# Scores in 32x64 tiles of 64 keys for five of eight chunks, and a late scaling in the first chunk

## The chip, the cores and the metric

The kernel runs on one core of a Trainium2 chip. The metric is device time in microseconds (us), the median of several executions. TensorE (PE; its weight loads are the profile's PEld) multiplies, VectorE (DVE), ScalarE (ACT) and GpSimd (POOL) work beside it, and SyncE (SP) issues the DMAs.

## What is computed

Two layers, each attention and an MLP, on 2048 tokens of 576 features. Attention has 32 heads of 18 features; a query sees itself and the 255 keys before it.

```python
def _A_ref(x, wqkv, wo):
    H = 32; Dh = D // H; W = 256
    qkv = (x @ wqkv).reshape(B, S, 3, H, Dh).transpose(2, 0, 3, 1, 4)
    scores = einsum("bhqd,bhkd->bhqk", q, k) * Dh ** -0.5
    mask = (i - j >= 0) & (i - j < W)
    return (softmax(where(mask, scores, -1e9)) @ v) ... @ wo
def _B_ref(x, w1, b1, w2, b2):
    return gelu(layernorm(x) @ w1 + b1) @ w2 + b2
x = x + _A_ref(layernorm(x)); x = x + _B_ref(layernorm(x)); both once more
```

## The kernel before

**Chunks and stages.** The work is cut into eight chunks of 512 tokens (four blocks of 128): chunks 0 to 3 are layer 1, chunks 4 to 7 layer 2. Attention of chunk k is interleaved with the MLP of chunk k - 1. A chunk's scores, exps, masks and P V products form three stages (`ea`, `eb`, `ec`) of 3, 3 and 2 of the 8 head groups (`CUTS`, line 566); the matmuls of the MLP and of the projections fill TensorE between them.

**Scores.** A head group is four heads, each on its own 32 partitions of `qT` and `kT`. `scores` (L946, its matmuls on L957) takes keys as the stationary side, 128 of them, and streams up to 384 queries; the four heads run as four 32x128 tiles at once. One call is a burst of 512 columns for each head, written into two pairs of PSUM banks. A chunk with a chunk before it needs three bursts for a head group: 1536 columns, in which 128x128 blocks on the edge of the mask are computed in full. Two exps on ScalarE (L964, 1024 elements per partition each) empty a burst into one of six slots of `pT`; GpSimd cuts the masked blocks to zero (affine_select, L984); `pv` (L991, matmuls on L1002) multiplies with V in four 128x32 tiles. Chunks 0 and 4 have no chunk before them and need fewer columns.

**Tile shapes.** Between such bursts TensorE works in other shapes: 64x128 in L880, L1085 and L1130, 128x128 in L821 and L840, 128x32 in L824 and L1002. `quad` (L819) writes the same product either as one wide 128x128 matmul (L821) or as four 128x32 ones (L824).

**Chunk 0.** Its LayerNorm (`ln_norm_T`, L756) subtracts the mean and multiplies by the reciprocal deviation `rstd` in one VectorE instruction (L761). `rstd` comes from GpSimd (L749, L751). With `pe=True`, TensorE transposes the row (L778) and ScalarE copies it out (L781). The projections follow (L840), and their results leave PSUM by copies on VectorE (L888, L901) or ScalarE (L898).

**What sets the order.** `Plan` collects tasks with the tensors that they read and write; the table `ORDER` gives each engine its tasks by number, in the order in which they are issued, and `BANKS` the PSUM bank of each. `schedule` (L248) turns them into queues with semaphores; it also chooses `wide` for `quad` and puts warming matmuls (L726) into gaps. Every engine issues in its written order.

Of the kernel before, what the change touches and what calls it, by code (L numbers as in the profile page):

```python
# [361 lines left out]
PACE = {"f": 16.0, "c": 65.0, "r": 100.0, "h": 18.5, "s": 33.0}  # L362
# [8 lines left out]
def spread(s):  # L371
    for x in s.split():
# [181 lines left out]
def build_kernel(nc, A_x, A_wqkv, A_wo, B_x, B_w1, B_b1, B_w2, B_b2, out):  # L554
    D = 576
# [24 lines left out]
    NQN = 6  # L580
    WB = 6
    TOPF = D - 512
    KF = 2


    CH = [(l, t, 4) for l in range(NL) for t in range(0, NT, 4)]
# [777 lines left out]
```

## Time and profile before

| | |
|---|---|
| median of 3 runs | 856.53 us (855.35 to 856.9) |
| span of the profiled execution | 853.7 us |
| median less that span | 2.8 us |
| PE / ACT / DVE / POOL busy | 842.8 / 598.3 / 383.2 / 368.6 us |
| matmuls recorded | 11549 |
| granted TensorE clock | 1.000 |

In rows of groups, the two numbers behind the first bar are the busy time in us and the mean duration in ns, and behind the second bar stands the idle time of the engine just before, with what ended it. In rows of a timeline the first two numbers are start and length in us, merged over the instructions counted by x; brackets hold the idle time before them. A shape such as 32\*128 is the tile: rows of the array, then columns.

### The profile page before, as it was taken

What the parts mean: (1) busy time and instruction counts of PE and PEld (TensorE: products, weight loads), DVE (VectorE), ACT (ScalarE), POOL (GpSimd) and SP (SyncE); (2) the same over time, 40 slices, a digit from 0 to 9 for tenths busy, and PEclk for the clock granted to TensorE, in tenths of its full rate; (3) what the DMA queues carried; (4) which work ended last, traced back from release to release, by engine and by line L of the source; (5) the groups of instructions that cost most, each with busy time, mean ns of one, the idle gap of its engine ahead of it and who ended that gap; (6) DMA issues with size and microseconds to landing.
All of it is one profiled execution on the core that took longest, in us unless ns stands there. A gap on an engine that the chain in (4) does not pass through costs nothing.

```text
span 853.7 us, 26814 instructions
## 1 busy us (share of the span) xinstructions
PE 842.8 (99%) x11549; PEld 513.0 (60%) x11549; DVE 383.2 (45%) x943; ACT 598.3 (70%) x736; POOL 368.6 (43%) x551
## 2 busy tenths in 40 slices
PE   9999999999999999999999999999999999999998
PEld 6555555656556566565566665766556656556556
DVE  7877224635237533564237633654324434153013
ACT  5888886968767678578734788548876688862740
POOL 3865644455245473166501763425644256332100
PEclk9999999999999999999999999999999999999999
DMA  9588376361594643936466636575447645254820
GB/s 227 82 159 184 127 203 153 76 190 41 171 173 94 187 136 93 194 56 159 144 196 118 160 83 168 64 191 118 132 137 157 164 118 157 101 178 119 292 84 28
DMA packets 181989, 119.76 MB, mean 140 GB/s; under 512 B 107504, under 2 KB 181872, under 8 KB 181872
## 3 DMA queue, kind: packets, MB, share of 16 engines
q1 hardware_dynamic: 181872, 118.05, 54.7%
q8 instruction: 91, 1.49, 0.7%
q14 instruction: 26, 0.21, 0.1%
HBM read 90.10 MB, written 2.36 MB: 108 GB/s over the span
## 4 chain that ended last, share of the span: by engine, by line
PE 95%; DVE 2%; ACT 1%; DMA 1%; issue 1%; POOL 0%; DVEq 0%
PE ps L1130 33%; PE ps L821 28%; PE ps L880 9%; PE ps L824 8%; PE ps L957 7%; PE ps L1002 5%; PE ps L1085 4%; PE ps L840 2%; ACT pT L964 1%; DMA xnTa<-xn 1%; DVE st_all L736 0%; DVE x_res L1067 0%; DVE xn L761 0%; DMA x_res<-in_A_x_dram 0%; DVE oq L1008 0%
## 5 line engine op out<-in xcount | busy, mean ns | idle before, releaser
L964 ACT ACTIVATE pT<-ps 128x1024 bf16<-128x1024 f32 (+1 forms) x372 | 346.0, 998 | 76.8 <-PE ps L957 76.1
L984 POOL TENSOR_SCALAR_AFFINE_SELECT pT<-pT 128x512 bf16<-128x512 bf16 (+2 forms) x360 | 278.7, 801 | 198.7 <-ACT pT L964 196.8
L1130 PE MATMUL ps<-xnTm,w_sb 64*128 64x512 bf16 x2592 | 291.1, 376 | 0.2 <-ACT pT L964 0.2
L1140 ACT ACTIVATE hT<-ps,b1col 128x512 bf16<-128x512 f32 x276 | 169.6, 690 | 141.6 <-PE ps L1130 141.1
L821 PE MATMUL ps<-w_sb,hT 128*128 128x288 bf16 x1626 | 215.2, 287 | 0.8 <-issue 0.8
L1130 PEld LDWEIGHTS ps<-xnTm,w_sb 64*128 64x128 bf16 x2592 | 125.2, 94 | 144.7 <-issue 6.1
L821 PEld LDWEIGHTS ps<-w_sb,hT 128*128 128x128 bf16 x1626 | 151.5, 98 | 56.1 <-issue 16.3
L1067 DVE TENSOR_TENSOR x_res<-ps,x_res 128x288 f32<-128x288 f32 x224 | 97.0, 449 | 166.5 <-PE ps L821 129.4
L1008 DVE STREAM_TRANSPOSE oq<-ps 128x512 f32<-128x512 f32 x64 | 45.8, 715 | 110.4 <-PE ps L1002 108.9
L880 PE MATMUL ps<-wqkv,xnTa 64*128 64x288 bf16 x1296 | 90.7, 283 | 1.1 <-DMA xnTa<-xn 0.6
L901 DVE CAST qn<-ps 128x288 bf16<-128x288 f32 x114 | 48.3, 449 | 91.5 <-PE ps L880 85.0
L880 PEld LDWEIGHTS ps<-wqkv,xnTa 64*128 64x128 bf16 x1296 | 61.5, 94 | 29.3 <-issue 2.7
L749 POOL TENSOR_SCALAR vtmp<-mv_all 128x1 f32<-128x1 f32 (+1 forms) x43 | 9.0, 209 | 153.4 <-DVE mv_all L740 141.3
L824 PE MATMUL ps<-w_sb,hT 128*32 128x288 bf16 x1944 | 68.3, 287 | 0.0
L957 PE MATMUL ps<-qT,kT 32*128 32x256 bf16 (+2 forms) x1248 | 63.0, 273 | 1.2 <-ACT pT L964 0.8
L824 PEld LDWEIGHTS ps<-w_sb,hT 128*32 128x32 bf16 x1944 | 49.6, 97 | 11.9 <-issue 4.2
L1145 POOL TENSOR_TENSOR x_res<-x_res,b2bc 128x576 f32<-128x576 f32 x32 | 40.7, 1286 | 35.1 <-ACT hT L1140 35.1
L888 DVE CAST vA<-ps 128x288 bf16<-128x288 f32 x64 | 27.5, 447 | 61.1 <-PE ps L880 58.9
L736 DVE BATCH_NORM_STATS2 st_all<-x_res 128x6 f32<-128x288 f32 (+1 forms) x128 | 53.3, 442 | 3.4 <-DMA x_res<-in_A_x_dram 3.2
L1002 PE MATMUL ps<-pT,vA 128*20 128x384 bf16 (+2 forms) x1440 | 50.1, 273 | 0.1
L957 PEld LDWEIGHTS ps<-qT,kT 32*128 32x128 bf16 x1248 | 19.2, 92 | 39.8 <-issue 20.6
L1085 PE MATMUL ps<-wo_sb,attT 64*128 64x288 bf16 x576 | 40.2, 283 | 0.9 <-DVE qn L901 0.5
(57 smaller groups left out, 462.0 us busy)
## 6 DMA issues: line engine op xcount, KB each, us to landing
w_sb<-in_B_w_dram SPq DMA_DIRECT2D x46, 864.0 KB, 6.1
w_sb<-in_B_w_dram SPq DMA_DIRECT2D x48, 768.0 KB, 5.7
w_sb<-in_B_w_dram SPq DMA_DIRECT2D x96, 48.0 KB, 3.6
out_dram<-x_res SPq DMA_DIRECT2D x16, 144.0 KB, 4.2
wqkv<-in_A_wqkv_dram SPq DMA_DIRECT2D x3, 576.0 KB, 5.0
x_res<-in_A_x_dram SPq DMA_DIRECT2D x3, 576.0 KB, 4.4
wqkv<-in_B_w_dram SPq DMA_DIRECT2D x2, 864.0 KB, 8.6
wo_sb<-in_A_wo_dram SPq DMA_DIRECT2D x4, 144.0 KB, 3.9
```

The costliest lines, as they stand in the source:

```text
L736: add("dve", lambda e, i=i, s=s: e.bn_stats(st_all[:, t, i, :], s[:, t, i * HB:(i + 1) * HB]), reads=res, writes=[f"st{t}_{i}"], cost=0.37 ...
L821: return e.matmul(bank(b)[:, 0:HB], lhs, rhs, start=start, stop=stop, skip_group_check=True)
L824: ins = e.matmul(bank(b)[32 * j:32 * j + 32, 0:HB], lhs[:, 32 * j:32 * j + 32], rhs, start=start, stop=stop, tile_position=(0, 32 * j), sk ...
L880: ins = e.matmul(bank(bs[o])[:, 0:HB], xnTa[r:r + 64, c, i * 128:(i + 1) * 128], wqkv[r:r + 64, c, col:col + HB], start=(c == 4), stop=(ph ...
L957: ins = e.matmul(two(bs[j // 2])[:, j % 2, col:col + nq * 128], k_of(T0 + so)[0][32 * j:32 * j + 32, g, :], qs[32 * j:32 * j + 32, g, qo * ...
L964: add("act", lambda e, h2=h2: e.activation(pT[:, sl, 2 * h2:2 * h2 + 2, lo:hi], two(bs[h2])[:, :, lo:hi], ACT.Exp, scale=SCALE), reads=[bs ...
L984: add("pool", lambda e, ap=ap, pat=pat, sgn=sgn, kind=kind: e.affine_select(ap, ap, pattern=pat, compare_op=(ALU.is_ge if kind == "d" else ...
L1002: ins = e.matmul(bank(bo)[32 * j:32 * j + VW, qo * 128:(qo + nq) * 128], vA[:, (T0 + so) % VS, 8 * j + g, :], pT[:, sl, j, col:col + nq * ...
L1067: add("dve", lambda e: e.tensor_tensor(x_res[:, t, sl], bank(b)[:, 0:HB], x_old[:, t, sl], ALU.add), reads=[b] + ([f"xin{t}"] if first els ...
L1085: ins = e.matmul(bank(bs[o])[:, 0:HB], attT[r:r + 64, c, i * 128:(i + 1) * 128], wo_sb[r:r + 64, c, o * HB:o * HB + HB], start=(c == 4), s ...
L1130: ins = e.matmul(bank(bks[i])[:, 0:n], w1_sb[r:r + 64, sls[i], col:col + 128], xnTm[r:r + 64, k % 2, c, 0:n], start=(c == 4), stop=(ph == ...
L1140: add("act", lambda e, ff=ff, hd=hd, bk=bk: e.activation(hd[:, 0:n], bank(bk)[:, 0:n], ACT.Gelu_apprx_tanh, bias=b1col[:, ff:ff + 1]), rea ...
```

## The change

**Scores.** For chunks 2, 3, 5, 6 and 7 (`HALF`) a new function `pair` treats two head groups at once. `halves` writes their scores in five bursts of 512 columns instead of six. A tile is now 32x64: half a key block is stationary, so each half meets only the 64-query steps that its own mask leaves, and two halves times four heads make eight tiles. A piece is four matmuls (one per head) with one half of keys. Two bursts of a pair hold four pieces, three hold six. An exp now empties a window of a burst into its place in `pT` (`exps`): 28 exps for a pair, 64 to 384 columns of two banks each, instead of 12. `cut` issues the same masks as before. Waits between exps, masks and P V go by cells of 64 columns (`cells`). The stages now hold 4, 2 and 2 head groups, and score pairs, projections and P V may use any PSUM bank.

**Chunk 0.** With `pe=True` the VectorE instruction only subtracts the mean; the drains behind the projections multiply by `rstd` (VectorE tensor_scalar or ScalarE mul) where they copied.

**Orders.** `ORDER` and `BANKS` are written anew. TensorE has 12490 matmuls instead of 11549. SP loads the tokens of chunk 1 ahead of the k weights.

The diff, cut to its core:

```diff
-    CUTS = ((0, 3, 6, 8), (0, 4, 8, 8))
+    CUTS = ((0, 4, 6, 8), (0, 4, 8, 8))
+    HALF = (2, 3, 5, 6, 7)
-    FILL = (7, 6, 5, 4)
-    OUT = (7, 6, 5, 4)
+    FILL = (7, 6, 5, 4, 3, 2, 1, 0)
+    OUT = (7, 6, 5, 4, 3, 2, 1, 0)
-    SC = (0, 2, 4)
+    SC = (0, 1, 2, 3, 4, 5, 6)
...
+        if pe:
+            add("dve", lambda e: e.tensor_scalar(xn[:, sl, 0:D], s[:, t, :], mv_all[:, t, 0:1], None, op0=ALU.subtract),
+                reads=res + [f"mv{t}"], writes=[f"xn{sl}"], cost=0.37, lat=0.14, prio=prio, port=True)
...
+        def drain(e, dst, src):
+            if k:
+                return e.tensor_copy(dst, src)
+            return e.tensor_scalar(dst, src, rstd[:, i:i + 1], None, op0=ALU.mult)
...
+    def exps(sl, bs, dst, src, n, prio):
+
+        for h2 in range(2):
+            add("act", lambda e, h2=h2: e.activation(pT[:, sl, 2 * h2:2 * h2 + 2, dst:dst + n], two(bs[h2])[:, :, src:src + n], ACT.Exp, scale=SCALE),
+                reads=[bs[h2]], writes=cells(sl, dst, dst + n, (h2,)), cost=0.07 + 2 * n * 0.00083, lat=0.17, prio=prio)
...
+    def halves(k, pieces, wins, prio):
...
+        def fn(e):
+            ins = None
+            for (g, so, u, q, n, col) in pieces:
+                for j in range(4):
+                    ins = e.matmul(two(bs[j // 2])[64 * u:64 * u + 64, j % 2, 64 * col:64 * (col + n)],
+                                   k_of(T0 + so)[0][32 * j:32 * j + 32, g, 64 * u:64 * u + 64], qs[32 * j:32 * j + 32, g, 64 * q:64 * (q + n)],
+                                   start=True, stop=True, tile_position=(32 * j, 64 * u), skip_group_check=True)
+            return ins
...
+        def edge(g, more):
+            unit(g, [(g, 0, 0, 0, 5, 1), (g, 0, 1, 1, 5, 2), (g, 3, 1, 7, 1, 7), (g, 3, 0, 6, 2, 6), (g, -2, 0, 0, 1, 0), (g, -2, 1, 0, 2, 0)],
+                 [(g, "X", 0, 6, 1), (g, "X", 6, 2, 0), (g, "Y", 0, 2, 6)], [(g, "X", "d", 0, 1), (g, "X", "o", 256, 2)] + more)
+        edge(a, [])
+        unit(a, [(a, 1, 0, 2, 5, 3), (a, 1, 1, 3, 4, 4), (a, -1, 1, 0, 4, 0), (a, -1, 0, 0, 3, 0)],
+             [(a, "Y", 2, 5, 3), (a, "Z", 0, 4, 0)], [(a, "Y", "d", 0, 2), (a, "Z", "o", 128, 1)])
+        unit(a, [(a, 2, 0, 4, 4, 0), (a, 2, 1, 5, 3, 1), (b, -1, 1, 0, 4, 4), (b, -1, 0, 0, 3, 4), (a, 1, 1, 7, 1, 0), (b, 1, 0, 2, 1, 7)],
+             [(a, "Z", 4, 4, 0), (a, "Y", 7, 1, 0), (b, "Z", 0, 4, 4), (b, "Y", 2, 1, 7)],
+             [(a, "Z", "d", 256, 1), (a, "Y", "o", 384, 1), (b, "Z", "o", 128, 1)])
+        done(a)
+        unit(b, [(b, 1, 0, 3, 4, 0), (b, 1, 1, 3, 5, 0), (b, 2, 0, 4, 4, 4), (b, 2, 1, 5, 3, 5)],
+             [(b, "Y", 3, 5, 0), (b, "Z", 4, 4, 4)], [(b, "Y", "o", 384, 1), (b, "Z", "d", 256, 1)])
+        edge(b, [(b, "Y", "d", 0, 2)])
+        done(b)
```

A piece is (head group, key block, half of keys, first query, number of queries, column), the last three in steps of 64; a window is (head group, slot, first column there, number, first column of the burst).

Three places of the order show it. First TensorE in attention stage `ea` of chunk 2, before: bursts of chunk 2 (L957) between MLP matmuls of chunk 0 (L821, L824).

```order
L957 MATMUL ps<-qT,kT 128x384 x4
L957 MATMUL ps<-qT,kT 128x128 x4
L821 MATMUL ps<-w_sb,hT 128x288 x18
L957 MATMUL ps<-qT,kT 128x384 x4
L957 MATMUL ps<-qT,kT 128x128 x4
L821 MATMUL ps<-w_sb,hT 128x288 x12
L957 MATMUL ps<-qT,kT 128x256 x8
L824 MATMUL ps<-w_sb,hT 32x288 x24
```

The same stage now (L1037 are the new bursts, L840 and L843 the MLP's wide matmuls and quads), the third to the fifth burst of the first pair:

```order
L1037 MATMUL ps<-qT,kT 64x320 x4
L1037 MATMUL ps<-qT,kT 64x256 x8
L1037 MATMUL ps<-qT,kT 64x192 x4
L840 MATMUL ps<-w_sb,hT 128x288 x12
L1037 MATMUL ps<-qT,kT 64x256 x4
L1037 MATMUL ps<-qT,kT 64x320 x4
L1037 MATMUL ps<-qT,kT 64x256 x4
L1037 MATMUL ps<-qT,kT 64x192 x4
L840 MATMUL ps<-w_sb,hT 128x288 x18
L1037 MATMUL ps<-qT,kT 64x320 x8
L1037 MATMUL ps<-qT,kT 64x64 x4
L1037 MATMUL ps<-qT,kT 64x128 x4
```

Bursts of 8 matmuls became bursts of 16 or 24. With the burst just ahead of these rows and the next one behind them, five bursts in a row stand with 66 wide matmuls (18, 12, 18 and 18), 72 quads and one P V group of 24.

ScalarE at the same place (L978 are the exps; before, its row in the stage was L964 with 128x1024 and x18):

```order
L978 ACTIVATE pT<-ps 128x2x384
L978 ACTIVATE pT<-ps 128x2x128
L978 ACTIVATE pT<-ps 128x2x384
L978 ACTIVATE pT<-ps 128x2x128 x3
L978 ACTIVATE pT<-ps 128x2x64
L978 ACTIVATE pT<-ps 128x2x256
L978 ACTIVATE pT<-ps 128x2x64
L978 ACTIVATE pT<-ps 128x2x256
```

One kind of exp became windows of different widths, each for two banks.

TensorE at the start, before: warming matmuls (L726), transposes of the first rows (L778), projections (L840).

```order
L726 MATMUL ps<-warm 128x256 x13
L778 MATMUL ps<-ident,xn 128x128 x5
L726 MATMUL ps<-warm 128x256 x5
L778 MATMUL ps<-ident,xn 128x128 x5
L840 MATMUL ps<-wqkv,xnTa 128x288 x20
L778 MATMUL ps<-ident,xn 128x128 x5
L840 MATMUL ps<-wqkv,xnTa 128x288 x25
```

And now (L741, L797, L859):

```order
L741 MATMUL ps<-warm 128x256 x8
L797 MATMUL ps<-ident,xn 128x128 x5
L741 MATMUL ps<-warm 128x256 x7
L797 MATMUL ps<-ident,xn 128x128 x10
L859 MATMUL ps<-wqkv,xnTa 128x288 x25
L797 MATMUL ps<-ident,xn 128x128 x4
L859 MATMUL ps<-wqkv,xnTa 128x288 x5
```

The third row of tokens is transposed ahead of the first projection instead of behind 20 of its matmuls, and the first 30 projections are q alone.

More of the change, by code (lines that the diff above doesn't have):

```diff
@@ L361 @@
 RING = 2048
-PACE = {"f": 16.0, "c": 65.0, "r": 100.0, "h": 18.5, "s": 33.0}
+PACE = {"f": 16.0, "c": 65.0, "r": 100.0, "h": 18.5, "s": 33.0, "q": 160.0}
+HALF_EXTRA = 0.05
 FETCH = 300
@@ L960, in scores @@
         rd = [f"{qname}{qo + i}" for (g, so, qo, nq, col) in parts for i in range(nq)] + [k_of(T0 + p[1])[1] for p in parts]
-        add("pe", fn, reads=rd, writes=bs, cost=sum(mm_cost(p[3] * 128) for p in parts), prio=prio, lat=0.15, alloc=bs, mode="r", after=[f"p{sl}h{h}" for h in range(2)] + [f"p{sl}m{m}" for m in range(3)])
         lo, hi = min(p[4] for p in parts), max(p[4] + p[3] * 128 for p in parts)
-        for h2 in range(2):
-            add("act", lambda e, h2=h2: e.activation(pT[:, sl, 2 * h2:2 * h2 + 2, lo:hi], two(bs[h2])[:, :, lo:hi], ACT.Exp, scale=SCALE),
-                reads=[bs[h2]], writes=[f"p{sl}h{h2}"], cost=0.07 + 2 * (hi - lo) * 0.00083, lat=0.17, prio=prio)
+        add("pe", fn, reads=rd, writes=bs, cost=sum(mm_cost(p[3] * 128) for p in parts), prio=prio, lat=0.15, alloc=bs, mode="r", after=cells(sl, lo, hi))
+        exps(sl, bs, lo, lo, hi - lo, prio)
         blk = {}
@@ L978, in scores @@
                 runs.append([blk[c], c, 1])
-        need = {}
-        for mi, (kind, col, nb) in enumerate(runs):
-            sgn = 1 if kind == "d" else -1
-            pat = [[0, 4]] + ([[0, nb]] if nb > 1 else []) + [[sgn, 128]]
-            ap = pT[:, sl, :, col:col + nb * 128]
-            add("pool", lambda e, ap=ap, pat=pat, sgn=sgn, kind=kind: e.affine_select(
-                ap, ap, pattern=pat, compare_op=(ALU.is_ge if kind == "d" else ALU.is_gt), fill=0.0, base=0, channel_multiplier=-sgn),
-                reads=[f"p{sl}h0", f"p{sl}h1"], writes=[f"p{sl}m{mi}"], cost=0.12 + 0.475 * nb, prio=prio)
-            for n in range(nb):
-                need[col + n * 128] = f"p{sl}m{mi}"
-        return sl, {p[4]: [f"p{sl}h0", f"p{sl}h1"] + list(dict.fromkeys(need[c] for c in range(p[4], p[4] + p[3] * 128, 128) if c in need)) for p in parts}
+        for kind, col, nb in runs:
+            cut(sl, kind, col, nb, prio)
+        return sl
+    def halves(k, pieces, wins, prio):
+        l, t0, nt = CH[k]
+        T0 = l * NT + t0
+        qs, qname = q_of(k)
+        bs = [Bank(SC, True), Bank(SC, True)]
+        def fn(e):
[6 more added lines that the diff above has]
+            return ins
+        rd = list(dict.fromkeys([f"{qname}{x // 2}" for (g, so, u, q, n, col) in pieces for x in range(q, q + n)] + [k_of(T0 + p[1])[1] for p in pieces]))
+        add("pe", fn, reads=rd, writes=bs, cost=512 / 2400.0 + 0.0023 * (len(pieces) / 2) + HALF_EXTRA, prio=prio, lat=0.15, alloc=bs, mode="q",
+            after=[c for (sl, dst, n, src) in wins for c in cells(sl, 64 * dst, 64 * (dst + n))])
+        for (sl, dst, n, src) in wins:
+            exps(sl, bs, 64 * dst, 64 * src, 64 * n, prio)
     def pv(k, g, todo, prio):
@@ L999, in fn @@
             ins = None
-            for n, ((_, so, qo, nq, col), sl, _) in enumerate(todo):
+            for n, ((_, so, qo, nq, col), sl) in enumerate(todo):
                 for j in range(4):
@@ L1005, in fn @@
             return ins
-        rd = list(dict.fromkeys([x for _, _, names in todo for x in names] + [f"v{(T0 + p[1]) % VS}h{o}" for p, _, _ in todo for o in range(2)]))
-        add("pe", fn, reads=rd, writes=[bo], cost=sum(mm_cost(p[3] * 128) for p, _, _ in todo), prio=prio, lat=0.2, mode="c", alloc=[bo])
+        rd = list(dict.fromkeys([x for p, sl in todo for x in cells(sl, p[4], p[4] + p[3] * 128)] + [f"v{(T0 + p[1]) % VS}h{o}" for p, _ in todo for o in range(2)]))
+        add("pe", fn, reads=rd, writes=[bo], cost=sum(mm_cost(p[3] * 128) for p, _ in todo), prio=prio, lat=0.2, mode="c", alloc=[bo])
         add("dve", lambda e: e.transpose(oq[:, 0:4 * nt, :].rearrange("p b c -> p (b c)"), bank(bo)[:, 0:nt * 128]),
@@ L1027, in pv, with pair, at, unit @@
                     reads=[f"aq{x}" for x in range(32 * c // DH, g + 1)] + (["ax0", "ax1"] if c == KD - 1 else []), writes=[f"aT{c}"], cost=0.6, lat=0.14, prio=prio - 3)
+    def pair(k, a, b, prio):
+        ss = {}
+        PARTS = {"X": ((0, 0, 3, 0), (-2, 0, 1, 384)), "Y": ((1, 1, 3, 128), (3, 3, 1, 0)), "Z": ((-1, 0, 2, 0), (2, 2, 2, 256))}
+        def at(g, w):
+            if (g, w) not in ss:
+                ss[g, w] = slots.popleft()
+            return ss[g, w]
+        def unit(g, pieces, wins, cuts):
+            PL.part = f".{g}"
+            halves(k, pieces, [(at(x, w), dst, n, src) for (x, w, dst, n, src) in wins], prio)
+            for (x, w, kind, col, nb) in cuts:
+                cut(at(x, w), kind, col, nb, prio)
+        def done(g):
+            pv(k, g, [((g,) + p, ss[g, w]) for w in "XYZ" for p in PARTS[w]], prio - 0.1)
+            for w in "XYZ":
+                slots.append(ss[g, w])
+        def edge(g, more):
[12 more added lines that the diff above has]
+        done(b)
+        PL.part = ""
     def E(k, gs, prio):
+        if k in HALF:
+            for n in range(0, len(gs), 2):
+                pair(k, gs[n], gs[n + 1], prio)
+            return
         todo = units_of(k, gs)
@@ L1048, in E @@
             PL.part = f".{u[0][0]}"
-            sl, names = scores(k, u, prio)
+            sl = scores(k, u, prio)
             flush()
@@ L1052, in E @@
             for p in u:
-                parts[p[0]].append((p, sl, names[p[4]]))
+                parts[p[0]].append((p, sl))
                 left[p[0]] -= 1
```

60 lines of the change are left out of this document (36 added, 24 removed), and 323 rows, old and new, of the table ORDER.

## The prediction

> **What bounds the kernel now.** I read the busy line of the page first, then the chain of work that ended last, then the engines' busy time by stretches.
>
> ```profile
> PE 842.8 (99%) x11549; PEld 513.0 (60%) x11549; DVE 383.2 (45%) x943; ACT 598.3 (70%) x736; POOL 368.6 (43%) x551
> PE 95%; DVE 2%; ACT 1%; DMA 1%; issue 1%; POOL 0%; DVEq 0%
> ...
> 0.00:20.00 20.00, 18.42 (x155) 13.19 (x155) 14.46 (x44) 11.46 (x20) 7.93 (x23) 1.00 1.01 234
> 20.00:100.00 80.00, 75.69 (x1135) 45.27 (x1138) 55.00 (x138) 68.25 (x94) 54.86 (x85) 1.00 0.69 141
> 100.00:800.00 700.00, 698.08 (x9850) 420.14 (x9844) 303.77 (x739) 503.45 (x604) 305.79 (x443) 1.00 0.54 140
> 800.00:853.70 53.70, 50.60 (x428) 34.45 (x424) 9.97 (x24) 15.16 (x22) 0.00 (x0) 1.00 0.33 108
> ```
>
> The window rows give the stretch, its length, then the busy time of PE, PEld, DVE, ACT and POOL. TensorE is busy 842.8 of 853.7 us, and 95% of the chain is its own. Between 100 and 800 us it idles 1.9 us in all; the other 9 us lie in the first 100 us and in the last 53. The granted clock is 1.00 in every row. So whatever happens after 100 us counts only if it changes TensorE's own work, or makes another engine late enough that TensorE must stop. Anything saved on ScalarE (70%), VectorE (45%) or GpSimd (43%) is worth nothing there.
>
> What that work costs is read from starts, not from durations, because matmuls overlap. The timeline rows show start, length, engine, line, tile shape and count:
>
> ```profile
> 330.18 0.40 PE L957 MATMUL ps<-qT,kT 32*128 32x384 bf16 x8
> 330.51 1.64 PE L821 MATMUL ps<-w_sb,hT 128*128 128x288 bf16 x12
> 332.09 0.40 PE L957 MATMUL ps<-qT,kT 32*128 32x384 bf16 x8
> ...
> 333.99 0.40 PE L957 MATMUL ps<-qT,kT 32*128 32x256 bf16 x8
> 334.32 0.83 PE L1002 MATMUL ps<-pT,vA 128*20 128x384 bf16 x24
> 334.98 0.91 PE L824 MATMUL ps<-w_sb,hT 128*32 128x288 bf16 x24
> 335.82 0.40 PE L957 MATMUL ps<-qT,kT 32*128 32x384 bf16 x8
> ...
> 803.28 11.93 PE L821 MATMUL ps<-w_sb,hT 128*128 128x288 bf16 x96
> 815.14 11.83 PE L1130 MATMUL ps<-xnTm,w_sb 64*128 64x512 bf16 x108
> ```
>
> Ninety-six wide matmuls take 815.14 - 803.28 = 11.86 us, twelve take 332.09 - 330.51 = 1.58. The slope is (11.86 - 1.58)/84 = 0.122 us for one, and what is left of the twelve is 1.58 - 12 x 0.122 = **0.11 us for the change of tile shape** behind them. The 24 P V matmuls (334.32 to 334.98) take 0.66 us and pay no such change, since the quads behind them have the same 128-row, 32-column tiles; their streaming alone, 2 x (384 + 128 + 256) columns with four tiles abreast, is 0.64 us at 2.4 columns per ns (the 288 columns of a wide matmul in 0.122 us give that rate). A score burst of 512 columns takes 330.51 - 330.18 = 0.33 us whatever follows it, so **0.22 us and a change**.
>
> **The change part by part.** Sums are made against the profiled execution: 853.7 us of span, 2.8 us below the median of 856.5; I carry that difference along.
>
> *Fewer bursts.* Five chunks x 8 head groups x 3 = 120 bursts of 32x128 tiles become 5 x 4 pairs x 5 = 100 of 32x64 tiles, each still 512 columns wide if its two column halves stream side by side. 20 x 0.22 = **-4.4 us**.
>
> *Fewer changes of shape.* Counted along TensorE's order, neighbours with different tile shapes stand at 410 places before and at 387 now. 23 x 0.11 = **-2.5 us**. Wide matmuls and quads change places (1898 wide and 2104 quad matmuls before, 1956 and 1872 now), at no cost: 24 quads take 335.82 - 334.98 - 0.11 = 0.73 us, as six wide ones do.
>
> *Thicker bursts.* A new burst holds 16 or 24 short matmuls where there were 8. The trace has no 32x64 tile, so this is bounded by the nearest rows.
>
> ```profile
> 330.18 0.12 PEld L957 LDWEIGHTS ps<-qT,kT 32*128 32x128 bf16 x8 [0.24 <-issue]
> ...
> 368.93 0.40 PE L957 MATMUL ps<-qT,kT 32*128 32x128 bf16 x12
> 369.26 1.64 PE L821 MATMUL ps<-w_sb,hT 128*128 128x288 bf16 x12
> ...
> L957 PEld LDWEIGHTS ps<-qT,kT 32*128 32x128 bf16 x1248 | 19.2, 92 | 39.8 <-issue 20.6 <-ACT pT L964 15.5 <-DVE x_res L1067 0.9
> ```
>
> From below: a burst of chunk 4 in three parts and 12 matmuls takes 0.33 us too, so more and shorter parts can be free: 0. From above: the third part on a tile must have its weights loaded after the second part has begun to stream, and one load lasts 92 ns. In the two edge bursts of a pair (queries 320, 64 and 128 wide on one half) that would end at 320/2.4 + 92 + 128/2.4 = 278 ns instead of 213, which is 65 more; in the others 11 at most. That is 32 ns on average. In between lies the program's order: matmuls start in order here, and in an edge burst the last 128 columns stand behind a 64-column piece that begins at column 448, so they end at 576 instead of 512, 27 ns later, 11 ns on average over the five. I add 14 ns because eight first matmuls start one after another instead of four: eight loads take 0.12 us where one takes 92 ns, so starts are about 4 ns apart. I take **25 ns x 100 = +2.5 us**, between the two ends, nearest to the order. What speaks against more is the three-part row.
>
> The Trainium skill has a rule against such a cut: "TensorEngine Tiling (Array Packing)", section "Instruction Overhead", gives each matmul about 60 cycles whatever its width, and advises not to take the tiling factor from a small dimension. The narrowest piece here is 64 columns, just above that, so by the rule the sum stays where it is; the trace shows no piece below 128 columns in a score burst.
>
> *More exps.* A pair's 12 exps become 28 with the same columns. ScalarE's pitch:
>
> ```profile
> 339.65 1.94 ACT L964 ACTIVATE pT<-ps 128x1024 bf16<-128x1024 f32 x2 [1.43 <-PE ps L957]
> ...
> 36.19 10.66 ACT L964 ACTIVATE pT<-ps 128x768 bf16<-128x768 f32 x15 [0.84 <-PE ps L957]
> ...
> 349.30 1.27 ACT L1140 ACTIVATE hT<-ps,b1col 128x512 bf16<-128x512 f32 x2 [3.78 <-PE ps L1130]
> 352.81 0.69 ACT L1140 ACTIVATE hT<-ps,b1col 128x512 bf16<-128x512 f32 x1 [2.25 <-PE ps L1130]
> ...
> L964 ACT ACTIVATE pT<-ps 128x1024 bf16<-128x1024 f32 x324 | 310.8, 1023 | 72.7 <-PE ps L957 72.4
> L964 ACT ACTIVATE pT<-ps 128x768 bf16<-128x768 f32 x48 | 35.2, 828 | 4.1 <-PE ps L957 3.7
> ```
>
> One 1024-element exp behind another costs 1.94 - 1.02 = 0.92 us, a 768-element one (10.66 - 0.83)/14 = 0.70: 0.85 ns per element and 0.05 us fixed. A pair then costs 12288 x 0.85 ns + 28 x 0.05 = 11.8 us against 11.0 before, and the 320 added instructions 16 us of ScalarE in all. The cover is TensorE's work between the bursts. In the stretch of the new order shown for chunk 2, five bursts in a row, with 28 exps, stand with 66 wide matmuls, 72 quads, 24 P V matmuls and ten changes: 5 x 0.245 + 66 x 0.122 + 18 x 0.122 + 0.66 + 1.1 = 13.2 us. ScalarE fits, with 1.4 us to spare, so **0**. If the fixed part is larger than (13.2 - 10.4)/28 = 0.10 us, the cover is gone; that is a rival below. GpSimd's cuts keep number and shape (244, 112 and 4): 0.
>
> *Chunk 0.* Centring no longer waits for the deviation, so the first two rows of tokens reach TensorE sooner. But the q weights land late:
>
> ```profile
> 2.18 4.17 SPq L676 DMA_DIRECT2D wqkv<-in_A_wqkv_dram  x7
> ...
> wqkv<-in_A_wqkv_dram SPq DMA_DIRECT2D x3, 576.0 KB, 5.0
> ...
> 6.60 0.43 DVE L761 TENSOR_SCALAR xn<-x_res,mv_all,rstd 128x576 bf16<-128x576 bf16 x1 [1.03 <-POOL rstd L751]
> ...
> 7.09 0.51 PE L778 MATMUL ps<-ident,xn 128*128 128x128 bf16 x5 [0.40 <-DVE xn L761]
> 7.54 0.49 PEld L840 LDWEIGHTS ps<-wqkv,xnTa 128*128 128x128 bf16 x5
> ```
>
> Issued at 2.18, landing 5.0 us later, they are there at about 7.2 us, and the first projection loads its tokens, the stationary side, at 7.54. What comes off (1.03 us of wait for the second row) is thus shut in by a DMA that stays where it was. The new order also puts the third row's transposes ahead of the projections, and x for chunk 1 ahead of the k weights in SP's queue; the k projections move behind all q ones, which gives back that delay. What is late next is the DMA: **0**, with 1 us either way. Five fewer warming matmuls only filled idle time.
>
> ```profile
> 4.33 0.57 POOL L751 TENSOR_TENSOR rstd<-vtmp,nhalf 128x1 f32<-128x1 f32 x1
> ...
> 8.39 0.46 DVE L901 CAST qn<-ps 128x288 bf16<-128x288 f32 x1
> ...
> L901 DVE CAST qn<-ps 128x288 bf16<-128x288 f32 x114 | 48.3, 449 | 91.5 <-PE ps L880 85.0 <-PE ps L821 3.3 <-PE ps L840 1.8
> ...
> L761 DVE TENSOR_SCALAR xn<-x_res,mv_all,rstd 128x576 bf16<-128x576 bf16 x16 | 7.0, 450 | 1.4 <-POOL rstd L751 1.4
> ```
>
> The drains of chunk 0 now wait for the deviation, with the next statistics and drains of VectorE queued behind them. GpSimd has the first at 4.90 us, the first drain comes at 8.39, so 3.5 us cover that wait. A scaled drain out of PSUM is not in the trace; the same 288 elements copied take 0.45 us and a scaled row of 576 out of memory 0.45, so I count 0, at most 18 x 0.1 us of a VectorE that is busy 72% of the first 20 us.
>
> Sum: -4.4 - 2.5 + 2.5 = **-4.4 us**, 853.7 to 849.3 of span, and **852.1 us** for the median.
>
> **The rivals.** *Loads of one row group go one after another (slower).* A burst of six pieces then needs six loads per row group. The quads bound one load from above: 24 loads of 32 columns in 0.73 us are 30.5 ns each, 61 ns for 64 columns. Six take 366 ns against 220, four take 244: (3 x 146 + 2 x 24)/5 = 97 ns per burst, +9.7 us, 856.5 - 6.9 + 9.7 = **859.3 us**. It decides from 69 ns per burst (6.9 us over 100), about 55 ns a load. For it: every load that shares rows in this trace is narrow. Against: the three-part burst, three loads per row group, shows nothing. The Trainium skill, "TensorE: Matmul & The Clock Gate", section "LDWEIGHTS (loading the stationary operand)", counts a load by its columns, 53 ns for 64, and lets loads overlap only across row groups; by that estimate six take 320 ns and the sum would come out near no change, 856 us. No run here shows such a load yet; that outcome lies in the no-change case below.
>
> *Column halves do not stream side by side where rows are cut too (slower).* +0.213 us per burst: 852.1 - 2.5 + 21.3 = **871 us**. The trace has four row groups abreast (scores) and four column groups abreast (P V), never both.
>
> *ScalarE becomes the pace (slower).* With gelu's fixed part, 1.27 - 0.69 - 512 x 0.85 ns = 0.145 us, a pair costs 14.5 us against 13.2 of TensorE; with two such pairs in each of five chunks +13 us, **865 us**. For exps the two rows above say 0.05.
>
> *The burst eats the gain (no change).* At 52 to 86 ns per burst the time is within 0.2% of before.
>
> *More than forecast.* Bursts as cheap as the three-part row and 1 to 2.5 us fewer waits in the first 100 us, where 5.9 us of TensorE's idle time lies and the order is new: **847 to 849.5 us**.
>
> **How the numbers follow.** Forecast, 849.5 to 854.6: 0.56. More: 0.10. No change, 854.8 to 858.2 (0.2%, about what a measurement of this kernel can tell from no change): 0.14. Loads in line: 0.08; ScalarE's pace: 0.08; halves in line: 0.04. Faster 0.67 with what the edges add, same 0.13, slower 0.20. The range, 847 to 861, takes in the low end and the load rival and leaves out 865 and 871.
>
> **What would show it.** From the start of a score burst to the next matmul of another shape 0.35 to 0.37 us, against 0.33: the load rival shows 0.4 to 0.5, halves in line 0.54. The exp rows: 128-element exps should follow each other at 0.16 us; at 0.25 ScalarE paces. TensorE's idle time between 100 and 800 us should stay near 2 us, and the first projection near 7.6. It would be wrong if waits of score matmuls on the exps appear in the list of waits, with more than 5 us.

## The result: slower, and the profile after

The changed kernel takes **859.24 us** (median of 5 runs, 858.48 to 859.99) where the kernel before takes 856.53 (5 runs beside it): a ratio of 1.0041, 95% interval 1.0028 to 1.0054, which is 3.5 us (the two medians by themselves differ by 2.7). Forecast were 852.1 us, so the time is 7.1 us above it, inside the range and on the other side of no change. The profiled execution has a span of 857.2 us, 3.5 above that of before. Every time on record here is about 1.7 us above its span, so the profiled execution before was some 1.1 us shorter than its median and the one after 0.3; 0.8 of these 3.5 us can come from that. All five executions and every profiled one had a granted clock of 1.000; executions at 0.996 to 0.998, which were six of eleven of the run on full tiles and five of seven of the run with two pieces below, took some 2 to 4 us longer, so for these two runs the time at 1.000 is given too.

The page of the changed kernel, its busy line and the shares of the chain of waits:

```profile
PE 843.1 (98%) x12490; PEld 525.2 (61%) x12490; DVE 391.0 (46%) x943; ACT 611.2 (71%) x1052; POOL 371.7 (43%) x551
...
q8 instruction: 99, 1.62, 0.8%
...
PE 93%; ACT 2%; DVE 2%; issue 1%; DMA 1%; POOL 1%; SPq 0%; DVEq 0%
```

TensorE is as busy as before (843.1 against 842.8 us) in a longer span, and 2% of the chain has gone from it to other engines. Its busy time says little of its work, since ends of matmuls are modelled. The same stretches as before, of the changed kernel:

```profile
0.00:20.00 20.00, 18.37 (x156) 13.22 (x156) 15.82 (x47) 10.51 (x19) 9.32 (x27) 1.00 0.93 234
20.00:100.00 80.00, 75.97 (x1086) 43.79 (x1084) 56.79 (x141) 68.20 (x93) 55.90 (x84) 1.00 0.77 143
100.00:800.00 700.00, 694.47 (x10800) 432.25 (x10794) 307.94 (x733) 515.88 (x917) 306.34 (x441) 1.00 0.56 142
800.00:857.20 57.20, 54.33 (x462) 35.98 (x458) 10.43 (x24) 16.61 (x26) 0.12 (x1) 1.00 0.24 77
```

From 100 to 800 us TensorE now idles 5.5 us, where it idled 1.9. That is only the part that shows as idle: a matmul of 288 columns is drawn 0.28 us long while the next starts 0.06 to 0.12 us later, so a wait of up to about 0.2 us hides under the drawn end of the last one. Reading starts instead, as the prediction did (the time from one group's start to the next, less the group's own columns, less 0.11 us where the shape changes), all waits of TensorE between 100 and 800 us come to **3.7 us before and 10.8 after**, of which

| waits of TensorE from 100 to 800 us | before | after |
|---|---|---|
| on its own product, between the two halves of a 64-row product | 1.35 (6 places) | 3.36 (15) |
| without any semaphore | 0.87 (2) | 2.50 (3) |
| on the exps of ScalarE | 0.34 | 1.43 |
| on the cuts of GpSimd | 0.16 | 0.78 |
| other engines and DMAs, and waits whose releaser the trace does not show | 0.94 | 2.74 |
| sum | 3.7 | 10.8 |

From 20 to 100 us the sum hardly moves (6.4 before, 6.6 after), and the first 20 us neither.

The longest waits by the waits of TensorE in that window, before:

```profile
PE ps L821 <- issue: 0.8, 1, 0.8
PE ps L880 <- DMA xnTa<-xn: 0.6, 1, 0.6
```

and after:

```profile
PE ps L1058 <- issue: 1.3, 2, 1.0
PE ps L1037 <- ACT pT L978: 0.8, 2, 0.5
PE ps L840 <- issue: 0.7, 1, 0.7
PE ps L1227 <- DVE x_res L1164: 0.4, 1, 0.4
PE ps L905 <- ACT pT L978: 0.2, 1, 0.2
PE ps L1227 <- DVE oq L1064: 0.2, 1, 0.2
PE ps L1058 <- POOL pT L987: 0.2, 1, 0.2
PE ps L840 <- DVE mv_all L755: 0.2, 1, 0.2
```

Two rows have become eight, none of them large: the scores wait for exps, P V for the cuts, the MLP for the residual on VectorE. "Issue" is a stop with nothing to wait for. One of them, and two bursts behind it, on the timeline of TensorE after:

```profile
299.27 0.55 PE L1058 MATMUL ps<-pT,vA 128*20 128x384 bf16 x9
300.85 0.61 PE L1058 MATMUL ps<-pT,vA 128*20 128x384 bf16 x15 [1.03 <-issue]
301.39 0.43 PE L1037 MATMUL ps<-qT,kT 32*64 32x320 bf16 x24
301.76 1.64 PE L840 MATMUL ps<-w_sb,hT 128*128 128x288 bf16 x12
303.45 0.42 PE L1037 MATMUL ps<-qT,kT 32*64 32x256 bf16 x16
303.80 0.42 PE L840 MATMUL ps<-w_sb,hT 128*128 128x288 bf16 x2
```

P V stops in the middle of a group of 24, after nine matmuls, for 1.03 us. The packets that bring instructions (the row q8 of the page, 1.62 MB in 99 packets, 16 KB each) offer a reason, no more than that: the last one ahead of the stop is recorded at 298.39 us, 401 instructions of TensorE (loads and matmuls) after the one before it, where 270 to 355 instructions lie between them around this place in a run without the stop (the first experiment below). But 427 lie between the packets at 185.13 and 196.27 us of this same run, and TensorE does not stop there. A burst of 24 matmuls takes 301.76 - 301.39 = 0.37 us to the next matmul of another shape, one of 16 takes 0.35; over all 100 the median is 0.359, against 0.33 before.

The waits on its own product are seen in the waits of the weight loads, 20 to 800 us. Before:

```profile
PEld ps L1085 <- PE ps L1085: 2.9, 10, 0.4
...
PEld ps L880 <- PE ps L880: 2.1, 7, 0.4
...
PEld ps L1130 <- PE ps L1130: 0.8, 4, 0.2
```

After:

```profile
PEld ps L1182 <- PE ps L1182: 4.8, 14, 0.4
...
PEld ps L905 <- PE ps L905: 4.1, 12, 0.4
...
PEld ps L1227 <- PE ps L1227: 0.8, 2, 0.6
```

A 64-row product is made in two halves of its rows, and the second adds to what the first has written. If nothing stands between the halves in TensorE's order, the second half's load waits for the first half's last result: 0.37 us for the load, 0.225 us for the stream of matmuls. The new order has this at 23 places from 20 to 800 us, the old one at 9.

### The profile page after: what moved, and what is told of

The parts are those of the page before. It is cut to its first block, busy times and chain, and to the rows that moved or that the text cites. A ratio compares the mean times of both kernels' runs of the same rounds, so it can differ in the third digit from the quotient of the medians.

```text
span 857.2 us, 28905 instructions
## 1 busy us (share of the span) xinstructions
PE 843.1 (98%) x12490; PEld 525.2 (61%) x12490; DVE 391.0 (46%) x943; ACT 611.2 (71%) x1052; POOL 371.7 (43%) x551
## 3 DMA queue, kind: packets, MB, share of 16 engines
q8 instruction: 99, 1.62, 0.8%
## 4 chain that ended last, share of the span: by engine, by line
PE 93%; ACT 2%; DVE 2%; issue 1%; DMA 1%; POOL 1%; SPq 0%; DVEq 0%
PE ps L1227 33%; PE ps L840 28%; PE ps L905 8%; PE ps L843 7%; PE ps L1058 5%; PE ps L1182 4%; PE ps L1037 4%; PE ps L1002 2%; ACT pT L978 2%; PE ps L859 2%; DMA kT<-qn 1%; POOL pT L987 1%; PE ps L741 0%; DVE oq L1064 0%; DVE xn L780 0%
## 5 line engine op out<-in xcount | busy, mean ns | idle before, releaser
L978 ACT ACTIVATE pT<-ps 128x512 bf16<-128x512 f32 (+5 forms) x692 | 363.7, 638 | 59.6 <-PE ps L1037 38.2
L987 POOL TENSOR_SCALAR_AFFINE_SELECT pT<-pT 128x512 bf16<-128x512 bf16 (+1 forms) x360 | 278.7, 798 | 218.9 <-ACT pT L978 217.4
L840 PE MATMUL ps<-w_sb,hT 128*128 128x288 bf16 x1674 | 220.0, 287 | 0.8 <-issue 0.7
L1227 PEld LDWEIGHTS ps<-xnTm,w_sb 64*128 64x128 bf16 x2592 | 130.0, 94 | 139.7 <-issue 7.2
L840 PEld LDWEIGHTS ps<-w_sb,hT 128*128 128x128 bf16 x1674 | 156.3, 98 | 52.5 <-issue 11.1
L885 DVE CAST qn<-ps 128x288 bf16<-128x288 f32 x104 | 44.0, 450 | 106.8 <-PE ps L905 102.1
L843 PE MATMUL ps<-w_sb,hT 128*32 128x288 bf16 x1752 | 61.1, 287 | 0.0
L843 PEld LDWEIGHTS ps<-w_sb,hT 128*32 128x32 bf16 x1752 | 44.1, 97 | 10.8 <-issue 3.9
L1037 PE MATMUL ps<-qT,kT 32*64 32x256 bf16 (+4 forms) x2080 | 42.7, 252 | 0.8 <-ACT pT L978 0.8
L1058 PEld LDWEIGHTS ps<-pT,vA 128*20 128x20 bf16 x1440 | 29.1, 91 | 18.5 <-issue 5.9
```

What stands on the lines that cost most here:

```text
L840: return e.matmul(bank(b)[:, 0:HB], lhs, rhs, start=start, stop=stop, skip_group_check=True)
L843: ins = e.matmul(bank(b)[32 * j:32 * j + 32, 0:HB], lhs[:, 32 * j:32 * j + 32], rhs, start=start, stop=stop, tile_position=(0, 32 * j), sk ...
L885: return e.tensor_copy(dst, src)
L978: add("act", lambda e, h2=h2: e.activation(pT[:, sl, 2 * h2:2 * h2 + 2, dst:dst + n], two(bs[h2])[:, :, src:src + n], ACT.Exp, scale=SCALE ...
L987: add("pool", lambda e: e.affine_select(ap, ap, pattern=pat, compare_op=(ALU.is_ge if kind == "d" else ALU.is_gt), fill=0.0, base=0, chann ...
L1037: ins = e.matmul(two(bs[j // 2])[64 * u:64 * u + 64, j % 2, 64 * col:64 * (col + n)], k_of(T0 + so)[0][32 * j:32 * j + 32, g, 64 * u:64 * ...
```

## The experiments

The question after the trace is whether those waits are the loss, or whether the bursts, ScalarE or chunk 0 are. The theory was: the work fell as forecast and the new order of the five engines, in which TensorE has no slack, gave it back in many small waits. Its rivals: the finer bursts cost more than their starts show; ScalarE is the pace; chunk 0's scaling holds up the start. In the edits "-" is the changed kernel, unless another is named. Each run stands beside the kernel before on its own chip (855.3 to 855.7 us there), so against the changed kernel I compare ratios, 0.001 of which are 0.86 us, and the spans of the profiled executions (857.2 for the changed kernel). A span is one execution, and its start varies: in the run with shorter exps, whose start is not touched, the matmuls at 20 us stand 1.1 us later than in the changed kernel.

**Bursts on full tiles.** Keys of a burst are all 128, in two column parts of 384 and 128, so eight matmuls instead of 16 or 24, everything else in the new order:

```diff
-            for (g, so, u, q, n, col) in pieces:
+            g, so = pieces[0][0], pieces[0][1]
+            for (c0, n) in ((0, 384), (384, 128)):
                 for j in range(4):
```

> The changed kernel in its own order, but each of the 100 new bursts streams its 512 columns as 8 matmuls in 32x128 tiles (one key block for all of them, so the scores of five chunks are wrong). Theory: the new bursts cost what their rows show, 0.359 us against 0.330, and the loss lies in waits of the new order. Then 100 x 0.029 = 2.9 us go, and up to 2.5 us more if the three stops without a semaphore (1.20, 0.44 and 0.86 us) come from fetching instructions, of which there are 1280 fewer matmuls: 853.8 to 856.3 us. Rival: the short matmuls cause the whole distance of 7 us to the forecast: 852 us.

Measured: 856.31 us, ratio to the kernel before 1.0015 (1.0005 to 1.0025); 855.43 us at a granted clock of 1.000. By the ratios that is 2.2 us under the changed kernel, by the spans (854.4) 2.8. It is still not under the kernel before, although TensorE's work is now 6.9 us less. Three things moved at once: the bursts are 100 x 0.029 = 2.9 us thinner, the stops without a semaphore (2.5 us) are gone with 1280 of the matmuls, and this wait is new, on the timeline:

```profile
346.71 0.83 PE L1066 MATMUL ps<-pT,vA 128*20 128x384 bf16 x24
349.75 1.26 PE L1235 MATMUL ps<-xnTm,w_sb 64*128 64x512 bf16 x10 [2.21 <-DMA w_sb<-in_B_w_dram]
```

The MLP waits for one load of w1 that SP issues behind three transposes of q and k; these wait for their own inputs. In the changed kernel TensorE comes to this place at 348.80 us, and the load has landed at 348.56, so there it costs nothing:

```profile
348.80 1.26 PE L1227 MATMUL ps<-xnTm,w_sb 64*128 64x512 bf16 x10
```

All waits from 100 to 800 us: 11.0 us, as many as in the changed kernel. So the larger loss is not in the bursts. What their thickness is worth by itself this run does not tell; the last two runs do.

**Two pieces on 32x64 tiles.** The bursts keep the new tile shape, but have two pieces of 512 columns, eight matmuls, instead of four or six pieces:

```diff
-            for (g, so, u, q, n, col) in pieces:
+            for u in range(2):
                 for j in range(4):
-                    ins = e.matmul(two(bs[j // 2])[64 * u:64 * u + 64, j % 2, 64 * col:64 * (col + n)], ...
+                    ins = e.matmul(two(bs[j // 2])[64 * u:64 * u + 64, j % 2, 0:512], ...
```

> The changed kernel with 32x64 tiles, but two pieces of 512 columns in each burst instead of four or six, so 8 matmuls (scores of five chunks wrong). If the 29 ns of a new burst come from the number of its pieces, a burst takes 0.33 us and the time is that of the full tiles, 853.8 to 856.3 us. If they come from the tile shape (eight tiles, or the change of shape to and from it), a burst stays at about 0.355 us and the time is 2.5 us longer than with full tiles. If the two column halves did not stream side by side, 0.54 us.

Measured: 859.29 us, 1.0044 (1.0029 to 1.0059), by the ratio level with the changed kernel. But the two executions at a granted clock of 1.000, one of them the profiled one (854.9 us of span), took 856.6 us, 2.3 us under the changed kernel and 0.5 over the full tiles by the spans, 1.2 over the full tiles by the times at 1.000. The burst, on the timeline:

```profile
299.82 0.42 PE L1046 MATMUL ps<-qT,kT 32*64 32x512 bf16 x8
300.18 1.64 PE L848 MATMUL ps<-w_sb,hT 128*128 128x288 bf16 x12
301.82 0.42 PE L1046 MATMUL ps<-qT,kT 32*64 32x512 bf16 x8
```

With eight matmuls, as in the kernel before, it takes 0.36 us (median 0.354). So about 24 of the 29 ns come with the 32x64 shape, and cutting it into six pieces adds 5. The in-order rule of the forecast, by which only edge bursts lose 27 ns, falls. Stops without a semaphore are gone here too (11210 matmuls instead of 12490). The expectation was 2.5 us more than with full tiles if the shape costs; the burst has that price, and 0.5 to 1.2 us of it show in the time.

**No wait between the halves.** Both halves of each 64-row product read one row group, so nothing has to be waited for:

```diff
-                                r = 64 * (o ^ ph)
+                                r = 64 * o
...
-                        ... mode="h", own=(ph == 1), ...
+                        ... mode="h", own=False, ...
```

> The changed kernel with both phases of a 64-row product on the same row group, which need no wait of TensorE on itself between the phases (half of the sum over features is taken twice and half left out). In the changed kernel's trace 23 such waits of 0.225 us stand between 20 and 800 us, 5.2 us in all. Theory: they are part of the loss, 859.2 - 5.2 = 854.0 us. Rival: what TensorE then reaches early is not ready, and the time is found again in waits for other engines: 857 to 859 us.

Measured: 857.77 us, 1.0027 (1.0016 to 1.0038): 1.2 us under the changed kernel by the ratios, 1.1 by the spans (856.1), where 5.2 us of waits went (23 x 0.225). Matmul by matmul against the changed kernel, its start is 0.7 us later at 20 us and its end 1.1 earlier, so 1.8 us came back from 20 us on. The edit does not slow the products themselves: eighteen matmuls of 288 columns take 1.10 us with it and, where nothing is waited for, without it. Of these 1.8 us, 1.5 lie ahead of 100 us, where 8 of the 23 waits stood (1.8 us); from 100 to 800 us, where the other 15 stood (3.4 us), only 0.3 came. So there most of the time is waited for again, as the rival of the expectation said. One place shows it. The weight loads of the changed kernel:

```profile
264.95 0.48 PEld L1182 LDWEIGHTS ps<-wo_sb,attT 64*128 64x128 bf16 x10 [0.20 <-issue]
265.80 0.36 PEld L1182 LDWEIGHTS ps<-wo_sb,attT 64*128 64x128 bf16 x8 [0.37 <-PE ps L1182]
266.35 0.48 PEld L1182 LDWEIGHTS ps<-wo_sb,attT 64*128 64x128 bf16 x10 [0.19 <-ACT pT L978]
267.20 0.36 PEld L1182 LDWEIGHTS ps<-wo_sb,attT 64*128 64x128 bf16 x8 [0.37 <-PE ps L1182]
```

and of the experiment, where the same function stands in L1190:

```profile
264.70 0.97 PEld L1190 LDWEIGHTS ps<-wo_sb,attT 64*128 64x128 bf16 x18 [0.20 <-ACT pT L986]
266.11 0.97 PEld L1190 LDWEIGHTS ps<-wo_sb,attT 64*128 64x128 bf16 x18 [0.43 <-ACT pT L986]
```

The two waits on the product itself are gone. But the second product also waits for ScalarE to empty its banks, and that wait grew from 0.19 to 0.43 us: TensorE came sooner, ScalarE didn't. Of 0.45 us removed here 0.21 are left.

**The same in the kernel before.**

```diff
-                                r = 64 * (o ^ ph)
+                                r = 64 * o
```

> The kernel before with both phases of a 64-row product on the same row group, so without TensorE's waits on itself (half of the sum over features is taken twice and half left out). Its trace has 9 such waits of 0.225 us between 20 and 800 us, 2.0 us. Theory: 856.5 - 2.0 = 854.5 us, so that 3.2 us less comes off here than from the changed kernel, and this is that much of the loss. Rival: the waits are found again elsewhere in both, and the distance between the two kernels stays at 2.7 us.

Measured: 854.44 us, 0.9990 (0.9979 to 1.0000). Nine such waits, 2.0 us, went, and 0.9 us of time by the ratio, 0.3 by the spans (853.4). Without these waits in either kernel the changed one is still longer, by 3.2 us by the ratios (1.0027 against 0.9990) and 2.7 by the spans, where it was 3.5 by both. So these waits are the smaller part of the distance, 0.3 to 0.8 us.

**Shorter exps.** Every exp of the five chunks empties half its columns:

```diff
-... pT[:, sl, 2 * h2:2 * h2 + 2, dst:dst + n], two(bs[h2])[:, :, src:src + n], ACT.Exp ...
+... pT[:, sl, 2 * h2:2 * h2 + 2, dst:dst + n // 2], two(bs[h2])[:, :, src:src + n // 2], ACT.Exp ...
```

> The changed kernel with each of the 560 new exps over half of its window only (half of the probabilities of five chunks are left over from earlier ones), so some 100 us less work for ScalarE. Theory: stops of TensorE for ScalarE, and for GpSimd's cuts behind it, cost 1.4 and 0.8 us between 100 and 800 us, and about as much again where the releaser is not told: 855.5 to 858 us. Rival (ScalarE has become the pace): 850 us or less. Rival (TensorE alone): 859 us.

Measured: 857.80 us, 1.0027 (1.0015 to 1.0038). ScalarE's line on the page, and TensorE's longest waits from 100 to 800 us:

```profile
PE 841.7 (98%) x12490; PEld 526.0 (61%) x12490; DVE 391.9 (46%) x943; ACT 511.7 (60%) x1052; POOL 373.1 (44%) x551
...
PE ps L913 <- DMA xnTa<-xn: 1.3, 1, 1.3
PE ps L848 <- issue: 1.1, 1, 1.1
PE ps L1067 <- issue: 1.0, 1, 1.0
```

A hundred us off ScalarE (611.2 to 511.7) are worth 1.2 us by the ratios and nothing by the spans (857.7; from 20 us on this execution is 0.6 us shorter than the changed kernel's). The waits on exps are gone from 100 us on (1.43 to 0.05 us), but a DMA of transposed tokens is waited for, and the sum of the waits stays at 10.8. ScalarE isn't the pace.

**All MLP products wide.** The quads become wide matmuls, which thins TensorE's instructions from 12490 matmuls to 11086 and adds 50 changes of shape:

```diff
-            t.wide[0] = x == "1"
+            t.wide[0] = True
```

(x is the choice of the changed kernel.)

> The changed kernel with every quad written as one wide matmul: 1404 matmuls and as many weight loads fewer, and 50 more changes of tile shape (437 against 387), which cost 50 x 0.11 = 5.5 us. Theory: the stops without a semaphore are late fetches of instructions, and they go, 2.5 us: 862.2 us, with no such stop in the trace. Rival: they have another cause and stay: 864.7 us.

Measured: 859.47 us, 1.0045 (1.0029 to 1.0062). By 50 x 0.11 TensorE has 5.5 us more to do, and the time moves by 0.3 us by the ratios, 0.2 by the spans (857.4). The place of the long stop above, on the timeline here:

```profile
300.04 0.83 PE L1066 MATMUL ps<-pT,vA 128*20 128x384 bf16 x24
300.80 0.43 PE L1045 MATMUL ps<-qT,kT 32*64 32x320 bf16 x24
```

P V runs through. With fewer instructions the stops without a semaphore are gone (2.5 us), a wait of 1.4 us for a transpose of k at 63 us is gone, and the waits from 100 to 800 us are 7.4 us instead of 10.8. So the 5.5 us of added work are offset for the most part by waits that went, 2.5 us of them the stops, which went with the thinner stream and not because work filled them. The stops behaved as the theory of the expectation said; neither of its times (862.2 and 864.7 us) came, since other waits went too.

**Chunk 0 scaled early.** Centring and scaling in one instruction again, and plain drains:

```diff
-            add("dve", lambda e: e.tensor_scalar(xn[:, sl, 0:D], s[:, t, :], mv_all[:, t, 0:1], None, op0=ALU.subtract),
+            add("dve", lambda e: e.tensor_scalar(xn[:, sl, 0:D], s[:, t, :], mv_all[:, t, 0:1], rstd[:, t:t + 1],
+                                                  op0=ALU.subtract, op1=ALU.mult),
...
-            return e.tensor_scalar(dst, src, rstd[:, i:i + 1], None, op0=ALU.mult)
+            return e.tensor_copy(dst, src)
```

> The changed kernel with chunk 0 as before: centred and scaled ahead of the transposes, drains that copy, and GpSimd's deviations in the order that this needs. Theory: the late scaling is worth nothing, since the q weights land at about 7.2 us: 859.2 us, within 0.5. Rival (it helps): 860 us or more. Rival (it costs, by waits of the drains): 858 us or less.

Measured: 860.70 us, 1.0059 (1.0042 to 1.0075). It isn't clean: the gaps of the start were filled with 44 warming matmuls instead of 17. Once more, with 17:

> The changed kernel with chunk 0 scaled ahead of its projections as before, and this time with the changed kernel's 17 warming matmuls (the first such run had 44, some 2.9 us of TensorE more, and took 860.7 us). If chunk 0's later scaling is worth nothing either way, as forecast: 859.2 us within 0.7. If scaling behind the projections saves start-up time that the new order relies on: above 860.5 us, with the first projection later than in the changed kernel. If it costs: below 858 us.

Measured: 861.86 us, 1.0078 (1.0062 to 1.0095). The first 14 us of TensorE in this run:

```profile
8.56 0.51 PE L810 MATMUL ps<-ident,xn 128*128 128x128 bf16 x5 [1.38 <-DVE xn L789]
9.55 0.51 PE L810 MATMUL ps<-ident,xn 128*128 128x128 bf16 x5 [0.48 <-DVE xn L789]
9.93 2.61 PE L872 MATMUL ps<-wqkv,xnTa 128*128 128x288 bf16 x20
13.66 0.54 PE L872 MATMUL ps<-wqkv,xnTa 128*128 128x288 bf16 x3 [1.12 <-ACT xnTa L813]
```

and in the changed kernel:

```profile
6.89 0.79 PE L797 MATMUL ps<-ident,xn 128*128 128x128 bf16 x10
7.54 3.26 PE L859 MATMUL ps<-wqkv,xnTa 128*128 128x288 bf16 x25
```

In the new order three rows must be normalised ahead of the first projection, which scaled early would start at 9.93 instead of 7.54 us. At 12 us the distance is 3.7 us, at the end 2.3 by the spans (859.5) and 3.2 by the ratios. The late scaling thus pays for the new order of the start; against the kernel before, whose order got its first projection at 7.58 with early scaling, it gains nothing.

**Three things at once.** The full tiles, no wait between the halves (both halves read one row group, and scores are of all 128 keys, as in the single runs), and the load of w1 ahead of three transposes:

```diff
-        "... 1714 1835 1715 1816 1821 1830 1615 1810 1849 ..."
+        "... 1714 1835 1715 1615 1816 1821 1830 1810 1849 ..."
```

> The changed kernel with three things taken off together: the bursts as eight matmuls on tiles of 128 rows (856.3 us alone), no wait between the two phases of the 64-row products (857.8 us alone, 1.5 below the changed kernel), and the one load of w1 that TensorE waited 2.26 us for at 349.75 us issued on SP ahead of three transposes instead of behind them. If each saving stands by itself: 856.3 - 1.5 - 2.3 = 852.5 us, below the kernel before. If what is freed in one place is waited for in the next, as in the runs with one of them: 855 to 856 us, level with the kernel before, and TensorE's waits from 100 to 800 us stay near 8 to 10 us although 5 us of causes are gone.

Measured: **852.70 us, 0.9968 (0.9957 to 0.9979)**. The savings stood: 6.3 us off the changed kernel by the ratios, 6.2 by the spans (851.0), which is what the parts gave or promised alone: 2.2 to 2.8 for the tiles, 1.1 to 1.2 for the halves, 2.2 for the load, which no run moved by itself and which is a wait of the full tiles and not of the changed kernel. The place of the 2.21 us wait, on the timeline:

```profile
346.20 0.83 PE L1066 MATMUL ps<-pT,vA 128*20 128x384 bf16 x24
346.97 1.25 PE L1235 MATMUL ps<-xnTm,w_sb 64*128 64x512 bf16 x10
```

The MLP follows P V without a wait. The waits from 100 to 800 us are still 8.7 us (transposes 2.1, exps 1.8, VectorE 2.6, cuts 1.5, the rest untold), as many as the second theory of the expectation had said, but its time, 855 to 856, was not what came.

**With the change's own bursts.** The same two last edits, and a rule for wide products that takes 15 more of them:

```diff
-FETCH_US = 5.4
+FETCH_US = 7.0
```

> The changed kernel with its own 32x64 bursts, no wait between the phases, the same SP move, and 15 more products of pT and vA in the wide form (344 instead of 329), which thins TensorE's instruction stream where it ran densest. The 15 wide forms cost about 0.8 us of work by the run with all of them wide (105 more for 5.5 us) and should take away the three stops without a semaphore (2.5 us in the changed kernel). If the savings stand: 859.2 - 1.5 - 2.5 + 0.8 = 856.0 us. If they are waited for elsewhere: 857.5 to 858.5 us.

Measured: 857.10 us, 1.0021 (1.0011 to 1.0030). By the ratios 1.7 us of the expected 3.2 stood, by the spans (854.4) 2.8. The stops without a semaphore are gone, and the waits from 100 to 800 us are 8.5 us. This run and the one ahead of it differ in the bursts and the 15 products; 4.5 us lie between them by the ratios, 3.4 by the spans; the thickness and the wide products are 2.9 + 0.8 = 3.7. Neither has stops without a semaphore, so here the thickness counts in full.

No run that computes the kernel's own result was faster than the kernel before. Not tried: the new bursts in the old order of the other work. The old places of exps, cuts and P V don't fit five bursts for six, so that would be a third order rather than a test of this one.

## Why the prediction was wrong, point by point

- *Fewer bursts, -4.4, and fewer changes of shape, -2.5 us.* Right, as far as it can be read. No run tests them by themselves; with the old kind of burst and two causes of waits off, the time falls 0.32% below the kernel before, so the gain is there to be had, if less than these 6.9 us.
- *Thicker bursts, +2.5 us.* Right in size (0.359 against 0.33 us, 2.9 us; the last two runs bear it out), wrong in its inside. I had split 25 ns into 14 for eight first matmuls and 11 for the order of pieces in edge bursts. The runs give 24 ns for the 32x64 shape whatever the number of pieces and 5 for four more pieces. The rivals on the bursts fell with it: loads of one row group in line would have shown 0.4 to 0.5 us, column halves in line 0.54. That the load rival's time, 859.3 us, is the one that came is chance.
- *More exps, 0.* Right in their own cost: in the trace after, more than 70 exps of 128 elements follow one another at 0.16 us, as forecast, and ScalarE's busy time grew by 12.9 us of 16. But "ScalarE fits, so 0" was too much said: the average fits, and single bursts waited, 1.1 us more than before.
- *Chunk 0, 0.* Right against the kernel before (first projection at 7.58 us there and 7.54 now). In the new order it is worth 2.3 to 3.2 us, which that order uses up.
- *The step that failed* is the one that is not in the sum: that TensorE's idle time from 100 to 800 us should "stay near 2 us". Idle as the trace draws it, it went from 1.9 to 5.5 us. I counted the shapes of the new order and not its neighbours. Read from starts, the waits went from 3.7 to 10.8 us: 2.0 us of waits between halves that now stand next to each other, 1.6 us of stops without a semaphore as the matmuls grew from 11549 to 12490, 1.7 us for exps and cuts, 1.8 for the rest. Work -6.9 + 2.9 = -4.0, these waits +7.1, together +3.1 of the 3.5 us by which the span grew. This is read from the starts in the two traces. Taking waits away bears out a part of it: without the waits between halves and the stops, and with its own bursts, the changed kernel is 1.7 us shorter by the ratios, 2.8 by the spans. No rival named this. The order could have shown part of it ahead of the run: which halves stand side by side is in its rows.
- *What would make it wrong*: I had named waits of score matmuls on exps, above 5 us. They were 1.4 at most. The waits came from everywhere, each small.

What stays open: how much of each wait is a loss of its own. Of the 5.2 us of waits between halves some 1.2 came back (1.8 without the start), and 5.5 us of added work cost 0.3 as 2.5 us of stops went with it. That the load of w1 gave all its 2.2 us follows by subtraction, not from a run of its own. One place was shown where a wait moves to the next producer (0.24 us of 0.45). That the whole order is bound that way, by producers on the other engines at many places, is argued from it and not shown.

## What to carry to other kernels

When TensorE is 98% busy in a hand-written order, a change that takes work off it is worth that work less the waits of the new order, and the order must be read for them: a product whose second half adds to the first needs other work between its halves (0.225 us here, 23 places). Price a new tile shape by a row of that shape: more small matmuls cost little each, but the shape cost 24 ns for a burst, and in the runs with the most instructions stood stops that no semaphore explains. And a wait is not worth its length: 5.2 us of waits taken away gave 1.2, and 5.5 us of work added, which took 2.5 us of stops with it, cost 0.3.

## What the runs showed of the hardware that was not expected

- A burst of 32x64 tiles takes 24 ns longer than one of 32x128 tiles with as many matmuls and columns (0.354 against 0.330 us), and six pieces instead of two add 5 ns.
- TensorE stops in the middle of a group with no semaphore to wait for: 1.20, 0.44 and 0.86 us at 300.85, 591.8 and 649.83 us. At the first, 401 of its instructions lie between two of the 16 KB packets that bring them; 427 lie between two others (185.13 and 196.27 us) without a stop. The kernel before, with 11549 matmuls, has one such stop, 0.82 us at 648.83. In the runs with 11086 to 11212 matmuls there was no such stop, and in the one with 12222 none either, whose 15 wide products were put where the stream was densest. So fewer matmuls go with fewer stops, if not strictly; that a late packet is the cause is a guess, and wasn't tried by itself.
- The weight loads of a burst of six pieces, six on each row group with 64 columns each, do not line up behind one another: one is drawn 0.10 us long, and all 24 take 0.25 us from the first start to the last end.
